# Moving the score gathers of five heads in every chunk from SyncE's DMA queue to GpSimd's

## The chip, the cores and the metric

The kernel runs on one core of one Trainium2 chip. The metric is the device time of one execution in microseconds. Three runs before the change gave a median of 945.39 us (945.13 to 953.41).

## What is computed

Attention with a mixing of the heads before and after the softmax ("talking heads"), and behind it a gated feed-forward layer. Cut to what matters:

```python
batch, n_heads, seq, head_dim = 4, 12, 448, 64        # q, k, v in float32
scores = matmul(q, k.T) / sqrt(head_dim)
scores = einsum('bhij,hg->bgij', scores, w_pre)       # mixes the 12 heads
attn   = exp(scores - max(scores)); attn = attn / (sum(attn) + 1e-09)
attn   = einsum('bhij,hg->bgij', attn, w_post)        # mixes them again
x      = matmul(attn, v)  ->  (batch * seq, 768)
xn = x / rms(x) * rms_g
out = (silu(xn @ w_gate) * (xn @ w_val)) @ w_out      # 768 -> 1536 -> 768
```

## The kernel before, in words

The program is one long list of instructions whose order is written out by hand (the function `part_a` for attention, `part_b` for the feed-forward layer). Each engine takes its instructions strictly in that order and waits on semaphores for what it needs.

Attention is cut into 16 chunks `n`, four for each batch element, of 120 query rows each (100 in every fourth). Each chunk is worked off in 6 steps (5 in every fourth), 92 steps in all. A chunk passes through these stages:

- `qk_mm(n, hp)`, L123: TensorE multiplies q and k for a pair of heads into two PSUM tiles.
- `qk_evac(n, hp, j)`, L126 to L150: the scores of head h = 2 hp + j are copied from PSUM to an SBUF tile `st` (8 buffers), for the even head by ScalarE (L136) and for the odd one by VectorE (L134). Then a DMA, the *gather*, moves `st` into `r`, the tile of the whole chunk (three such tiles, used in turn): the 120 score rows of a head go to 10 partitions, 13 apart, 12 rows to each. So the 12 heads of a group of query rows come to stand on neighbouring partitions, where a matmul can mix them. A gather moves 10 x 12 x 448 floats (210 KB; 175 KB in the chunks of 100 rows). Head 11 takes two gathers of half that size, since it stands on other rows in the second half of the partitions. That makes 13 gathers a chunk.
- `premix(n, p)`, L158: TensorE mixes the heads out of `r` into the PSUM tiles `sp`. The first premix of a chunk needs all 13 gathers.
- `rowmax` (L164, VectorE) writes `nm`, `expo` (L171, ScalarE) writes `e`.
- `norm(n, p)`, L174 to L183: VectorE makes the reciprocals `rp` (L180), then GpSimd scales the post-mixing weights with them: two small TENSOR_SCALAR a step, which write `wn`.
- `postmix` (L197) multiplies `e` by `wn` into `pm`, one step later, and `evac_a` (L210, L212) copies that out.
- `av_mm` (L230), `av_copy` (L240, ScalarE), then `x_sum` (L249 to L259), five GpSimd operations twice a chunk, and `x_store` (L264), a DMA on SyncE's queue.

In one step t, TensorE takes premix(t), one `qk_mm` of the next chunk, postmix(t-1) and one `av_mm` of the chunk before. GpSimd takes, in this order: the jobs of the step (the q loads of L103 and the k loads of L96, which it issues as DMAs), the `wn` of step t, then `x_sum` where there is one. The six head pairs of chunk n + 1 are spread over the steps from two before the first of chunk n to three before the first of chunk n + 1, one pair a step (two in the first of them where chunk n has only 5 steps).

The line that picks a gather's queue is L149. For chunk 0 (n = 0) it deals the gathers out over three queues. For all others, n = 1 to 15, it takes `nc.sync`: 195 gathers, of which 75 are those of heads 1, 3, 5, 7 and 9.

Of the kernel before, what the change touches and what calls it, by code (L numbers as in the profile page):

```python
# [16 lines left out]
B, H, S, D = 4, 12, 448, 64  # L17
# [19 lines left out]
def attention_moe(ctx: ExitStack, tc, q, k, v, wpre, wpost, mask, ident, wgv, wo, rms_g, out):  # L37
    nc = tc.nc
# [87 lines left out]
    def qk_evac(n, hp, j):  # L126
        h, np_ = 2 * hp + j, PAIRS[n % NC]
        ps = qps[n, hp][j]
        if n or h >= 8:
            st = pq.tile([128, S], F32, name="st", tag="st", bufs=8)  # L130
        else:
            st = pro.tile([128, S], F32, name="st", tag="st", bufs=8)
        if j:
            nc.vector.tensor_copy(st, ps[:, :S])  # L134
        else:
            nc.scalar.activation(st, ps[:, :S], AF.Copy)  # L136
        for i, (lo, hi) in enumerate(((0, EARLY), (EARLY, 2 * np_)) if n == 0 else ((0, 2 * np_),)):
            w, at_ = RH * (hi - lo), 2 * RH * lo
            if h < H - 1:
                parts = [(h, 2 * RH, at_, 2 * w)]  # L140
            else:
                parts = [(h, RH, at_, w), (64, RH, at_ + w, w)]
            for row, k_, src, many in parts:
                dst = rt[n][row : row + (k_ - 1) * GAP + 1 : GAP, lo:hi]
                if i:
                    held.append((dst, st[src : src + many]))
                else:
                    turn = h if row < H else h + 1
                    eng = nc.sync if n or turn % 2 else nc.gpsimd if turn % 4 == 2 else nc.scalar  # L149
                    eng.dma_start(dst, st[src : src + many])  # L150

    def premix(n, p):
# [202 lines left out]
    def part_a(extra):  # L355
# [9 lines left out]
        for hp in range(H // 2):  # L365
            qk_mm(0, hp)
            for j in range(2):
                qk_evac(0, hp, j)
            if hp == 4:
                setup()  # L370
# [5 lines left out]
        for t in range(T + 24):  # L376
# [25 lines left out]
            for a in qk_at[t]:  # L402
                for j in range(2):
                    qk_evac(*a, j)
# [404 lines left out]
```

## Time and profile before

| what | value |
|---|---|
| time, median of 3 runs | 945.39 us |
| time of the profiled execution | 946.1 us |
| its span, first to last instruction | 944.3 us |
| TensorE (PE) busy | 869.3 us, 92% of the span |
| VectorE (DVE) busy | 551.4 us, 58% |
| GpSimd (POOL) busy | 383.9 us, 41% |
| ScalarE (ACT) busy | 344.1 us, 36% |
| mean DMA rate | 136 GB/s |

The time of the profiled execution is 1.8 us longer than its span (what lies around the first and last instruction) and 0.7 us above the median of the runs. In the rows, PE is the row of the matmuls and PEld that of the weight loads, which overlap them. SPq is SyncE's own queue, whose instructions are mostly DMA issues. The idle time of an engine stands in brackets with what ended it; "issue" there means that nothing the profile shows was waited for. Attention takes about the first 390 us.

### The profile page before, as it was taken

Reading aid. Unit: us, or ns where it says so; the run is one execution under the profiler, and the core shown is the slowest. Engines: PE = TensorE matmul, PEld = TensorE weight load, DVE = VectorE, ACT = ScalarE, POOL = GpSimd, SP = SyncE. Lnnn points to the kernel's source line nnn. Section 1 sums busy time; section 2 is a strip of 40 time slices with the busy share of each in tenths; the row PEclk is TensorE's granted clock in tenths of the full one; section 3 lists DMA queues with packets and bytes.
Section 4 is the critical chain, followed back from the end, with each engine's and each line's share of the span. In section 5 each row is a group of like instructions: output and inputs, shape, how many; then the busy total and the mean of one; then the engine's idle time right before and its main releaser. Section 6 shows DMA issues by size and latency. Waiting matters only on the chain.

```text
span 944.3 us, 29156 instructions
## 1 busy us (share of the span) xinstructions
PE 869.3 (92%) x12344; PEld 735.4 (78%) x12344; DVE 551.4 (58%) x959; ACT 344.1 (36%) x806; POOL 383.9 (41%) x531
## 2 busy tenths in 40 slices
PE   4798888898898897789999999999999989999998
PEld 1476666576666675678999999999999969999997
DVE  4576677777766674449545664459989868211100
ACT  2566665666666676621211111111111223311200
POOL 4335444444544436634554444444656613000000
PEclk8999999999999999899999999999999989999999
DMA  7765676667655743452321222314332364532010
GB/s 202 203 179 169 187 201 189 195 188 220 187 176 173 205 119 115 140 166 73 107 99 51 82 96 96 106 48 146 130 130 89 123 214 143 190 105 88 30 39 30
DMA packets 72765, 128.18 MB, mean 136 GB/s; under 512 B 19975, under 2 KB 62213, under 8 KB 72635
## 3 DMA queue, kind: packets, MB, share of 16 engines
q1 hardware_dynamic: 68342, 113.53, 38.7%
q0 software_dynamic: 3616, 12.02, 4.6%
q8 instruction: 97, 1.59, 0.7%
q10 hardware_dynamic: 677, 0.77, 0.3%
q14 instruction: 33, 0.27, 0.1%
HBM read 63.77 MB, written 22.95 MB: 92 GB/s over the span
## 4 chain that ended last, share of the span: by engine, by line
PE 62%; DVE 15%; DMA 8%; issue 6%; POOL 5%; ACT 3%; SPq 1%; DVEq 0%; POOLq 0%; ACTq 0%
PE pm L197 6%; PE po L521 6%; PE po L522 6%; PE po L520 6%; PE sp L158 6%; PE av L230 5%; PE qk L123 4%; PE pv L521 4%; PE pv L520 4%; PE pg L522 3%; PE pv L522 3%; PE pg L521 3%; PE pg L520 3%; DMA r<-st 3%; DVE wa L425 3%
## 5 line engine op out<-in xcount | busy, mean ns | idle before, releaser
L171 ACT ACTIVATE e<-sp,nm 128x448 f32<-128x448 f32 x180 | 112.6, 631 | 120.2 <-DVE nm L164 120.2
L197 PEld LDWEIGHTS pm<-wn,e 60*64 60x64 f32 x5152 | 112.1, 134 | 56.4 <-POOL wn L183 26.8
L164 DVE TENSOR_REDUCE nm<-sp 128x1 f32<-128x448 f32 x180 | 104.1, 619 | 73.7 <-PE sp L158 70.3
L197 PE MATMUL pm<-wn,e 60*64 60x60 f32 x5152 | 112.8, 221 | 20.9 <-issue 11.9
L183 POOL TENSOR_SCALAR wn<-wk,rp 128x60 f32<-128x60 f32 x180 | 55.1, 318 | 185.2 <-DVE rp L180 172.7
L158 PE MATMUL sp<-r,wk_pre 64*64 64x448 f32 x720 | 107.9, 557 | 20.2 <-DMA r<-st 10.8
L123 PE MATMUL qk<-k,q 64*64 64x448 f32 x768 | 111.6, 560 | 13.3 <-ACT st L136 8.4
L230 PE MATMUL av<-a,v 64*64 64x120 f32 (+3 forms) x3072 | 98.9, 251 | 9.5 <-issue 6.5
L230 PEld LDWEIGHTS av<-a,v 64*64 64x64 f32 x3072 | 87.6, 134 | 13.2 <-issue 9.7
L520 PE MATMUL pg<-x,wh 128*128 128x448 f32 x264 | 97.0, 367 | 0.0
L520 PE MATMUL pv<-x,wh 128*128 128x448 f32 x264 | 96.7, 366 | 0.0
L521 PE MATMUL pv<-x,wh 128*128 128x448 f32 x264 | 96.7, 366 | 0.0
L522 PE MATMUL pg<-x,wl 128*128 128x448 f32 x264 | 96.7, 366 | 0.0
L522 PE MATMUL pv<-x,wl 128*128 128x448 f32 x264 | 96.6, 366 | 0.0
L521 PE MATMUL pg<-x,wh 128*128 128x448 f32 x264 | 96.6, 366 | 0.0
L453 POOL TENSOR_TENSOR wl<-wc,wh 128x768 fp32r<-128x768 f32 x26 | 49.6, 1907 | 110.0 <-ACT wh L452 110.0
L452 ACT ACTIVATE wh<-wc 128x768 fp32r<-128x768 f32 x26 | 22.0, 847 | 193.2 <-DVE wc L428 193.2
L551 POOL TENSOR_TENSOR g<-g,u 128x448 f32<-128x448 f32 x48 | 62.0, 1292 | 62.6 <-DVE u L550 51.1
L123 PEld LDWEIGHTS qk<-k,q 64*64 64x64 f32 x768 | 43.1, 137 | 49.1 <-ACT st L136 20.7
L504 DVE TENSOR_TENSOR x<-hraw,x 128x448 fp32r<-128x448 f32 x48 | 33.1, 730 | 78.8 <-ACT x L503 78.7
L210 DVE COPY a<-pm 128x420 f32<-128x420 f32 x92 | 54.9, 597 | 30.5 <-PE pm L197 30.1
L134 DVE COPY st<-qk 128x448 f32<-128x448 f32 x96 | 59.1, 616 | 12.6 <-PE qk L123 12.3
(126 smaller groups left out, 1729.9 us busy)
## 6 DMA issues: line engine op xcount, KB each, us to landing
r<-st SPq DMA_DIRECT2D x121, 210.0 KB
wraw<-in_wgv SPq DMA_DIRECT2D x20, 768.0 KB
hd<-sg SPq DMA_DIRECT2D x48, 224.0 KB
hraw<-hd SPq DMA_DIRECT2D x48, 224.0 KB
wraw<-in_wo SPq DMA_DIRECT2D x12, 768.0 KB
r<-st SPq DMA_DIRECT2D x44, 175.0 KB
v<-in_v SPq DMA_DIRECT2D x24, 256.0 KB
q<-in_q POOLq DMA_DIRECT2D x28, 192.0 KB, 4.7
```

Source lines behind the costliest of these rows:

```text
L123: nc.tensor.matmul(ps[j][m, :S], qt[n][sl, hp, m], kt[n // NC, hp][sl], start=True, stop=True)
L134: nc.vector.tensor_copy(st, ps[:, :S])
L158: nc.tensor.matmul(o, wk_pre[sl], rt[n][sl, 2 * p + v_], start=True, stop=True)
L164: nc.vector.tensor_reduce(t, ps[:, :S], AX.X, ALU.max, negate=True)
L171: nc.scalar.activation(e, ps[:, :S], AF.Exp, bias=nmx.pop((n, p, u)), accum_out=sm[n, p][:, u : u + 1])
L183: nc.gpsimd.tensor_scalar(wn[n, p][:, u], wk, r[:, u : u + 1], 1.0, ALU.mult, ALU.mult)
L197: nc.tensor.matmul(o, e[u_][sl, j : j + JT], w[sl, u_], start=True, stop=True)
L230: nc.tensor.matmul(x, vt[b, hp][sl, j, c_], a, start=(c_ == 0), stop=(c_ == JC - 1))
L520: nc.tensor.matmul(ps, a, xh[:, kk], start=(i == 0), stop=False)
L521: nc.tensor.matmul(ps, a, xl_[:, kk], start=False, stop=False)
L522: nc.tensor.matmul(ps, a2, xh[:, kk], start=False, stop=(i == n - 1))
L551: nc.gpsimd.tensor_tensor(g, g, u, ALU.mult)
```

## The change

Gathers of chunks 1 to 15 whose head is odd and below 11 (`j` is 1 and `row` is below 11) are issued by GpSimd. All others stay on SyncE's queue, and chunk 0 is as it was.

```diff
                     turn = h if row < H else h + 1
-                    eng = nc.sync if n or turn % 2 else nc.gpsimd if turn % 4 == 2 else nc.scalar
+                    if n:
+                        eng = nc.gpsimd if j and row < H - 1 else nc.sync
+                    else:
+                        eng = nc.sync if turn % 2 else nc.gpsimd if turn % 4 == 2 else nc.scalar
                     eng.dma_start(dst, st[src : src + many])
```

The new lines push everything behind them down by three: L150 is L153 in the kernel after, L183 is L186, L249 is L252. The order of work on TensorE, VectorE and ScalarE is the same in both kernels.

On GpSimd, in the last three steps of chunk 1, around the first `x_sum` of the program (r_112 is the tile of chunk 3, k_1 and k_2 are key tiles of the next batch element, xt and sum belong to chunk 0's output), before:

```order
L96 DMA k_1_883<-in_k 128x448
L183 TENSOR_SCALAR wn<-wk,rp 128x60 x4
L249 TENSOR_TENSOR xt_980<-xt_980,xt_981 128x360
L250 TENSOR_TENSOR xt_981<-xt_980 128x360
L254 TENSOR_TENSOR xt_981<-xt_981 128x120
L256 TENSOR_TENSOR sum_1058<-xt_981 128x120
L96 DMA k_2_1061<-in_k 128x448
L183 TENSOR_SCALAR wn<-wk,rp 128x60 x2
```

And after:

```order
L96 DMA k_1_883<-in_k 128x448
L186 TENSOR_SCALAR wn<-wk,rp 128x60 x2
L153 DMA r_112<-st 10x10x448
L186 TENSOR_SCALAR wn<-wk,rp 128x60 x2
L252 TENSOR_TENSOR xt_980<-xt_980,xt_981 128x360
L253 TENSOR_TENSOR xt_981<-xt_980 128x360
L257 TENSOR_TENSOR xt_981<-xt_981 128x120
L259 TENSOR_TENSOR sum_1058<-xt_981 128x120
L96 DMA k_2_1061<-in_k 128x448
L153 DMA r_112<-st 10x10x448
L186 TENSOR_SCALAR wn<-wk,rp 128x60 x2
```

A gather now stands directly ahead of the two `wn` of its step, and behind the `x_sum` and the loads of the step before.

On SyncE's queue, the gathers of chunk 1 (r_113) and the first of chunk 2 (r_114) with the loads of v between them, before:

```order
L150 DMA r_113<-st 10x12x448 x10
L107 DMA v_0_433<-in_v 128x512
L107 DMA v_1_435<-in_v 128x512
L150 DMA r_113<-st 10x12x448
L150 DMA r_113<-st 5x12x448 x2
L107 DMA v_2_505<-in_v 128x512
L107 DMA v_3_507<-in_v 128x512
L150 DMA r_114<-st 10x12x448 x2
```

And after:

```order
L153 DMA r_113<-st 10x12x448 x5
L107 DMA v_0_433<-in_v 128x512
L107 DMA v_1_435<-in_v 128x512
L153 DMA r_113<-st 10x12x448
L153 DMA r_113<-st 5x12x448 x2
L107 DMA v_2_505<-in_v 128x512
L107 DMA v_3_507<-in_v 128x512
L153 DMA r_114<-st 10x12x448
```

Five of the ten whole gathers have gone from the queue; the last three of the chunk (head 10 and the two parts of head 11) stand where they stood, behind two loads of v.

## Rows read from the trace of the kernel before

**Rows 1.** Windows by stage: each engine's busy us (instructions), granted clock, DMA share, GB/s.

```profile
core 0: us, PE busy (x) PEld busy (x) DVE busy (x) ACT busy (x) POOL busy (x), PEclk, DMA share, GB/s
40.00:352.00 312.00, 273.23 (x8413) 209.00 (x8409) 214.95 (x537) 199.99 (x531) 142.62 (x318) 0.99 0.64 184
390.00:944.00 554.00, 540.67 (x2758) 492.48 (x2750) 298.48 (x344) 101.90 (x176) 197.03 (x146) 0.99 0.32 104
```

**Rows 2.** Waits of PE, 40 to 352 us: total us, times, longest.

```profile
PE pm L197 <- issue: 11.3, 12, 2.0
PE av L230 <- issue: 6.3, 8, 2.2
PE sp L158 <- issue: 4.8, 3, 2.1
PE pm L197 <- POOL wn L183: 3.3, 7, 1.0
PE sp L158 <- DMA r<-st: 3.2, 3, 1.2
PE sp L158 <- DMA v<-in_v: 2.6, 1, 2.6
```

**Rows 3.** Waits of SyncE's queue, 40 to 352 us, the longest three.

```profile
SPq L150 <- ACT a L212: 108.7, 55, 4.4
SPq L150 <- ACT xt L240: 35.9, 15, 4.7
SPq L150 <- DVE nm L164: 21.3, 41, 1.0
```

**Rows 4.** Tile r: issues of gathers, ns min/median/max, first and last start.

```profile
L150 SPq DMA_DIRECT2D r<-st x201: 742/756/1676, 7.1 to 352.3; - x101
L150 POOL DMA_DIRECT2D r<-st x3: 556/594/782, 8.9 to 12.9; - x3
```

**Rows 5.** GpSimd's groups, 40 to 352 us: the k loads, busy us, mean ns.

```profile
L96 POOL DMA_DIRECT2D k<-in_k x18 | 10.6, 587 | 0.0
```

**Rows 6.** Timeline of POOL, 180 to 190 us: start, length, work [idle before].

```profile
181.70 0.60 POOL L183 TENSOR_SCALAR wn<-wk,rp 128x60 f32<-128x60 f32 x2 [5.87 <-DVE rp L180]
182.26 0.95 POOL L249 TENSOR_TENSOR xt<-xt,xt 128x360 f32<-128x360 f32 x1
...
185.08 0.59 POOL L96 DMA_DIRECT2D k<-in_k  x1
185.71 0.60 POOL L183 TENSOR_SCALAR wn<-wk,rp 128x60 f32<-128x60 f32 x2
...
188.38 0.60 POOL L183 TENSOR_SCALAR wn<-wk,rp 128x60 f32<-128x60 f32 x2 [1.54 <-DVE rp L180]
```

**Rows 7.** Timeline of DVE, the same stretch.

```profile
183.10 0.62 DVE L134 COPY st<-qk 128x448 f32<-128x448 f32 x1
...
184.41 0.17 DVE L180 RECIPROCAL rp<-t 128x2 f32<-128x2 f32 x1
```

**Rows 8.** Timeline of PE, the same stretch.

```profile
182.52 1.03 PE L197 MATMUL pm<-wn,e 60*64 60x60 f32 x55
...
186.09 1.08 PE L197 MATMUL pm<-wn,e 60*64 60x60 f32 x55 [0.20 <-POOL wn L183]
```

**Rows 9.** Timeline of POOL: first and last of twelve late wn.

```profile
68.15 0.60 POOL L183 TENSOR_SCALAR wn<-wk,rp 128x60 f32<-128x60 f32 x2
...
348.49 0.60 POOL L183 TENSOR_SCALAR wn<-wk,rp 128x60 f32<-128x60 f32 x2
```

**Rows 10.** Timeline of PE: the postmix behind each of these two.

```profile
68.62 1.10 PE L197 MATMUL pm<-wn,e 60*64 60x60 f32 x51
...
348.86 1.08 PE L197 MATMUL pm<-wn,e 60*64 60x60 f32 x55
```

**Rows 11.** Chain that ended last, 36 to 47 us: start, us, what.

```profile
37.55 8.16 DMA r<-st
```

**Rows 12.** Timeline of PE, 37 to 46 us: chunk 1's first premix.

```profile
43.81 0.93 PE L158 MATMUL sp<-r,wk_pre 64*64 64x448 f32 x2 [2.65 <-DMA v<-in_v]
```

**Rows 13.** Timeline of SyncE's queue, up to 75 us: chunk 1's last gathers.

```profile
23.49 10.10 SPq L150 DMA_DIRECT2D r<-st  x10
33.63 1.72 SPq L107 DMA_DIRECT2D v<-in_v  x2
35.86 2.43 SPq L150 DMA_DIRECT2D r<-st  x3
```

## The prediction

> **What bounds the kernel now.** I read the windows by stage first, then the waits of PE, then the timelines of POOL, DVE and PE side by side. The windows show that the change can act in one stage only: from 390 us to the end PE is busy 540.67 of 554 us and no gather runs there [rows 1]. In the 312 us from 40 to 352, where nearly all the moved gathers are issued (the last gather of all starts at 352.3 [rows 4]), PE is busy 273.23 us, so some 39 us of idle time is all there is to win. DMA is at 0.64 of its 16 engines there, POOL is busy 142.62 us [rows 1].
>
> The waits of PE say what that idle time is. 22.4 us in 23 waits (11.3 + 6.3 + 4.8) end in "issue", nothing that the profile shows; 3.3 us in 7 end when POOL has made `wn`; 3.2 us in 3 end with a gather, and 2.6 us in one are put down to a load of v [rows 2]. That last one is chunk 1's first premix [rows 12], which reads no v: I count it as gathers, since the chain of waits has a gather in flight from 37.55 us for 8.16 us just there [rows 11]. So PE waits 5.8 us for gathers in this stage, and 3.3 us for POOL.
>
> SyncE's queue is not short of time. It waits 108.7 + 35.9 + 21.3 us at gathers for work of ACT and DVE [rows 3], more than half the stage; a gather costs it 756 ns to issue [rows 4].
>
> POOL has a pattern that matters more. In most steps it sits idle until DVE has made the reciprocals, as before the `wn` at 181.70 (5.87 us) and 188.38 (1.54 us). In the step behind an `x_sum` it does not: the `wn` at 185.71 starts without idle time, straight behind the sums (from 182.26) and a load of k [rows 6], 1.1 us after the reciprocal was done (184.41 + 0.17) [rows 7], and PE has to wait for it [rows 8].
>
> **What the change removes.** 75 issues of some 756 ns leave SyncE's queue, 57 us [rows 4]. Since that queue waits for data far longer than this, I cost the removal at nothing by itself. At chunk 1, the one place where the queue runs packed, ten gathers take it 10.10 us to 33.59; it then issues two loads of v and still waits 0.5 us, until 35.86, for the scores of head 10 [rows 13]. So the last gathers of the chunk cannot start earlier for being behind five instead of ten. What can get shorter is their way: 5 of a chunk's 13 gathers go through another queue. The bounds are no gain and all 5.8 us of PE's waits for gathers; I take the share of the gathers moved, 5/13 of 5.8, which is 2.2 us.
>
> The Trainium skill speaks against any such gain: "DMA: Bandwidth & Descriptors", section "Issuing engines are not separate DMA queues", says that transfers run on the same 16 DMA engines whichever engine issued them, and that another issuer saves only the time of issuing. No row before shows a full gather from POOL. By that rule this term is nothing, and the sum below would be 5.0 us slower instead of 2.8.
>
> **What it adds on POOL.** An issue of a DMA holds POOL for 587 ns with k loads of 224 KB [rows 5], and for 556 to 782 ns (594 in the middle) with the three half-sized gathers of chunk 0 [rows 4]. No full gather from POOL is in the trace. The lower bound is 556 ns, the upper bound twice the longest of the half-sized, 1.56 us; I take 0.59 us, as the k loads are of the same size as a gather.
>
> The gather also waits, for DVE's copy of `st`. Queued behind it on POOL are the two `wn` of the step, any `x_sum` and the next loads; PE waits for the `wn`. In an ordinary step this costs nothing. The copy of `st` ends at 183.72, the reciprocal at 184.58, and a `wn` starts some 0.1 to 0.2 us after that [rows 6, 7]: about 1.0 us in which POOL has nothing to do, against 0.59. Even past it there is a little room: PE took the `wn` of 181.70 at 182.52, 0.82 us after its start [rows 6, 8], where 0.38 would have done (185.71 to 186.09).
>
> In the step behind an `x_sum` there is no such gap. Of the 79 steps of this stage, 19 have a `wn` that starts within 0.1 us of the work before it on POOL. Three of them get no gather (head pair 5 is due there, which stays with SyncE). Four are taken by PE only 0.85 to 2.0 us after their start, so 0.59 us more finds room there. Twelve are left whose `wn` PE takes 0.37 to 0.47 us after the start, as fast as it can [rows 9, 10]. There the gather's 0.59 us stands in full between the sums and the `wn`, and PE's postmix starts later by it: 12 x 0.59 = 7.1 us.
>
> Not all of it reaches the end. PE has 23 "issue" waits in 312 us, one per 13.6 us; a delay in the step ahead of one (a step is 312 / 79 = 3.9 us) only shortens it. I take 3.9 / 13.6, about 0.3, as absorbed: 7.1 x 0.7 = 5.0 us. In the first 40 us POOL gets chunk 1's five gathers; PE there waits at chunk 1's premix anyway [rows 12], which hides a few tenths in the `wn` of chunk 0.
>
> **The sum.** 946.1 us of the profiled execution + 5.0 - 2.2 = 948.9. Its time is 0.7 us above the median of the runs (945.4), so I predict 945.4 + 2.8 = 948.2 us. A measurement of this kernel tells about 1% (9.5 us) from no change, so this is within it.
>
> **Rivals.**
> *Nothing is left.* The late `wn` are absorbed more often than I reckon, or PE gets back all 5.8 us of its waits for gathers. For it: every gather that leaves the queue also leaves the way of head 11's two, which come last. Against it: the twelve rows where PE takes `wn` at once. Time 945.4 + 5.0 - 5.8 = 944.6, or less with more absorbed.
> *POOL becomes the limit.* A full gather costs POOL not 0.59 but, by its size, twice the longest half-sized one, 1.56 us. The gap of an ordinary step is about 1.0 us, and PE leaves about 0.4 more, so this decides from about 1.4 us an issue on. Then the twelve late steps cost 12 x 1.56 x 0.7 = 13.1 us and the some fifty ordinary ones about 0.15 us each, 7.5 us: 945.4 + 20.6 - 2.2 = 963.8. For it: the one issue of 782 ns. Against it: the k loads, at 587 ns for as many bytes.
> *The transfers get room.* At a share of 0.64 [rows 1] the DMA engines are often busy, and a gather from 10 partitions to 120 or back may load some engines more than others, which no view here shows. If sending five of 13 another way evens that out, PE's 5.8 us for gathers go, and with them half of the 22.4 us of "issue", should those be code that arrives late for the same reason: 945.4 + 5.0 - 5.8 - 11.2 = 933.4. For it: the 8.16 us that a gather was in flight [rows 11]. Against it: "issue" waits have no cause in the profile. The Trainium skill has a rule for it ("DMA: Bandwidth & Descriptors", section "Why a DMA increments its semaphore by 16 and not by 1"): queues of SP put a transfer of k shares on the lowest-numbered k engines, GpSimd's on k engines from a cursor that goes round. No row before shows single engines.
>
> **Chances.** My forecast 0.57, nothing left 0.22, POOL the limit 0.13, room for the transfers 0.08. The forecast's own range is 942 to 952.5 (the 7.1 us from a third to all, the gain from 5.8 us to none). For 8 in 10 I go from 940 to 957, the lower end on the side of the third rival, the upper one what an issue of about 1.2 us would make (12 x 1.2 = 14.4 us, less the gain). Faster by over 1% (below 936) takes most of the third rival, 0.06; slower (above 954.8) the second, 0.13; the rest, 0.81, is within.
>
> **What would show it.** In the profile after, POOL should have some 75 more DMA issues of about 0.59 us; PE's waits for `wn` in the stage should grow from 3.3 to near 10 us, at the steps behind an `x_sum`; PE's waits for gathers should shrink from 5.8 to some 3.6 us; the stage should end about 3 us later and the rest stay. I am wrong if an issue costs POOL above 1 us, if `wn` waits appear in ordinary steps, or if "issue" on PE moves by more than 5 us.

## The result and the profile after

The changed kernel takes 959.22 us (median of 20 runs, 946.87 to 968.40), the kernel before on the same chip 947.56 us. The ratio is 1.0122, 95% interval 1.0088 to 1.0157: slower by 1.2%, some 11.6 us. The forecast was 2.8 us slower; its range reached to 957.

Single runs of one kernel spread by 6 to 22 us, and part of that is TensorE's mean granted clock, which each run reports. So beside each ratio I give a difference "at equal clock": over 301 runs of all kernels below, a straight line puts 7.7 us (+-1.2) on each 0.01 of clock, the rest spreads by 3.4 us, and the kernels' means are compared along that line. The changed kernel stands at +11.4 +-1.6 us by it. (A change that itself lowers the clock is flattered by this; where that matters I say so. The ratios leave out the runs over 1.5% above the fastest of their kernel, while the line takes all 301; without those runs no difference moves by more than 1.7 us, except that of `loads_sp_memset`, which loses three of its six runs and goes to -7.8 +-3.7.)

The waits of PE in the stage, 40 to 365 us since the last gather now starts at 364.3 (total us, times, longest), answer to [rows 2]:

```profile
PE av L233 <- issue: 12.9, 11, 2.2
PE pm L200 <- issue: 9.4, 10, 2.4
PE pm L200 <- POOL wn L186: 9.0, 10, 1.5
PE qk L123 <- ACT st L136: 5.5, 3, 1.8
PE sp L161 <- DMA v<-in_v: 2.9, 3, 2.3
PE qk L123 <- issue: 1.3, 1, 1.3
...
PE sp L161 <- DMA wraw<-in_wgv: 0.7, 1, 0.7
...
PE sp L161 <- issue: 0.2, 1, 0.2
PE sp L161 <- DMA r<-st: 0.2, 1, 0.2
```

Of the kernel before, beside [rows 2], one more "issue" wait:

```profile
PE qk L123 <- issue: 0.8, 1, 0.8
```

Waits for `wn` rose from 3.3 to 9.0 us, all ten of them in steps where a gather stands behind an `x_sum`. Waits on transfers fell from 5.8 to 3.8 us (2.9 + 0.7 + 0.2); two kernels below that move no gather, memset_pool and memset_early, have 3.7 and 2.2 us, so the fall need not come from the change. "Issue" stands at 23.8 (before 23.2, the 22.4 of the prediction and the 0.8 at `qk`). Read this way, every step of the prediction seems to come out. Yet the stage ends later by far more than 3 us. The windows answer to [rows 1], the stage stretched to where it ends now:

```profile
core 0: us, PE busy (x) PEld busy (x) DVE busy (x) ACT busy (x) POOL busy (x), PEclk, DMA share, GB/s
...
40.00:365.00 325.00, 280.85 (x8439) 211.42 (x8439) 216.10 (x541) 201.69 (x534) 188.12 (x390) 0.98 0.64 178
```

The same work of the stage takes PE 13 us more than in the 312 us before. From chunk 1's first `wn` (51.3 us before, 51.2 after) to the last step ahead of the last gather (351.1 and 363.9) I get 299.9 and 312.7 us; what follows takes 593.2 and 593.6 us. Of the 12.8 us, PE's idle time makes 6.8 (35.0 to 41.8). Another 5.1 is clock, which fell to one half (1.2 of 2.4 GHz) three times, each time behind an "issue" wait of about 2 us, and not once in this stretch of the profile before. One such fall in the windows, the first at full clock with PE hardly busy:

```profile
118.00:121.00 3.00, 0.59 (x33) 0.45 (x30) 1.02 (x2) 1.77 (x5) 0.64 (x1) 0.99 0.91 266
121.00:124.40 3.40, 3.40 (x70) 3.07 (x73) 0.83 (x3) 0.61 (x1) 1.18 (x3) 0.51 0.50 145
124.40:128.00 3.60, 3.60 (x115) 2.69 (x108) 2.90 (x7) 2.20 (x6) 3.29 (x7) 1.00 0.26 76
```

That share is mostly chance: over the runs the mean clock is 0.9763 against 0.9778, worth 1.2 us.

Tile r on GpSimd, and that engine's groups in the stage (busy us, mean ns, idle before), answer to [rows 4] and [rows 5]:

```profile
L153 SPq DMA_DIRECT2D r<-st x126: 748/781/1647, 7.1 to 364.3; - x126
L153 POOL DMA_DIRECT2D r<-st x78: 553/620/782, 8.9 to 360.6; - x78
```

```profile
L153 POOL DMA_DIRECT2D r<-st x70 | 43.9, 627 | 77.9 <-DVE st L134 75.5 <-issue 1.5 <-DVE t L181 0.2
...
L96 POOL DMA_DIRECT2D k<-in_k x18 | 11.1, 617 | 0.1
```

75 more issues of 0.63 us, as reckoned (0.59). GpSimd waits 75.5 us at them for VectorE's copies of `st`, in time that it had. A late step looks like [rows 6] with one more line (start, length, work):

```profile
68.33 0.43 POOL L259 TENSOR_TENSOR sum<-xt 128x120 f32<-128x120 f32 x1
68.70 0.62 POOL L96 DMA_DIRECT2D k<-in_k  x1
69.32 0.61 POOL L153 DMA_DIRECT2D r<-st  x1
69.97 0.60 POOL L186 TENSOR_SCALAR wn<-wk,rp 128x60 f32<-128x60 f32 x2
```

The queues at work (packets, MB, share of 16 engines' span), first of the kernel before, then after:

```profile
q1 hardware_dynamic: 68342, 113.53, 38.7%
q0 software_dynamic: 3616, 12.02, 4.6%
q8 instruction: 97, 1.59, 0.7%
```

```profile
q1 hardware_dynamic: 58992, 98.12, 33.3%
q0 software_dynamic: 9616, 27.45, 10.3%
q8 instruction: 97, 1.59, 0.7%
```

q1 is SyncE's queue, q0 GpSimd's: 15.4 MB went over. The last line, 97 packets of 16 KB, will matter.

### The profile page after: what moved, and what is told of

The parts are those of the page before. It is cut to its first block, busy times and chain, and to the rows that moved or that the text cites. A ratio compares the mean times of both kernels' runs of the same rounds, so it can differ in the third digit from the quotient of the medians.

```text
span 957.5 us, 29206 instructions
## 1 busy us (share of the span) xinstructions
PE 875.9 (91%) x12344; PEld 737.6 (77%) x12344; DVE 552.3 (58%) x959; ACT 345.0 (36%) x806; POOL 430.3 (45%) x606
## 4 chain that ended last, share of the span: by engine, by line
PE 63%; DVE 13%; POOL 7%; issue 7%; DMA 7%; ACT 2%; SPq 0%; DVEq 0%; POOLq 0%; ACTq 0%
PE pm L200 6%; PE po L524 6%; PE po L525 6%; PE po L523 6%; PE sp L161 5%; PE av L233 5%; PE qk L123 4%; PE pg L523 4%; PE pv L523 4%; PE pg L525 4%; PE pv L525 4%; PE pv L524 4%; PE pg L524 4%; DVE wa L428 2%; DMA wraw<-in_wgv 2%
## 5 line engine op out<-in xcount | busy, mean ns | idle before, releaser
L200 PEld LDWEIGHTS pm<-wn,e 60*64 60x64 f32 x5152 | 109.7, 136 | 69.5 <-POOL wn L186 39.3
L153 POOL DMA_DIRECT2D r<-st x78 | 48.8, 626 | 91.6 <-DVE st L134 76.4
L186 POOL TENSOR_SCALAR wn<-wk,rp 128x60 f32<-128x60 f32 x180 | 54.7, 313 | 62.6 <-DVE rp L183 56.2
```

Of the source, the lines that this page charges most:

```text
L186: nc.gpsimd.tensor_scalar(wn[n, p][:, u], wk, r[:, u : u + 1], 1.0, ALU.mult, ALU.mult)
L200: nc.tensor.matmul(o, e[u_][sl, j : j + JT], w[sl, u_], start=True, stop=True)
```

## The experiments

Three theories stood at first. **A**: GpSimd's time at the issues holds up `wn`, as predicted, only oftener. **B**: a gather that goes through GpSimd's queue costs something by its way, whatever time GpSimd has. **C**: the change also alters which of the eight `st` buffers a tile gets, since the pool hands out the one that is free first. In the built programs a buffer comes back after exactly 8 tiles before, after 4 to 11 in the changed kernel. "Ordinary" places are 52 of the 75, "late" ones the 23 behind an `x_sum`.

All runs, with their interval and the difference at equal clock (95%):

| kernel | ratio to before | at equal clock, us |
|---|---|---|
| again (before itself) | 1.0004 (0.9970 to 1.0038) | +0.7 +-2.0 |
| the change | 1.0122 (1.0088 to 1.0157) | +11.4 +-1.6 |
| early_only | 1.0092 (1.0060 to 1.0123) | +9.1 +-2.2 |
| late_only | 1.0364 (1.0319 to 1.0410) | +29.7 +-2.9 |
| memset_pool | 1.0030 (0.9991 to 1.0068) | +3.8 +-2.0 |
| after_rot | 1.0087 (1.0053 to 1.0120) | +9.0 +-2.6 |
| before_slots_of_after | 0.9992 (0.9959 to 1.0025) | +0.1 +-2.0 |
| early_rot | 1.0067 (1.0036 to 1.0098) | +7.5 +-2.0 |
| late_rot | 1.0084 (1.0049 to 1.0119) | +7.3 +-2.0 |
| memset_early | 1.0013 (0.9987 to 1.0040) | +0.2 +-2.0 |
| copy_early | 1.0309 (1.0262 to 1.0357) | +20.8 +-3.1 |
| loads_sp | 0.9979 (0.9947 to 1.0012) | -5.1 +-2.0 |
| after_loads_sp | 1.0064 (1.0024 to 1.0104) | +7.0 +-2.0 |
| both_early | 1.0119 (1.0078 to 1.0159) | +12.7 +-2.8 |
| scalar_early | 1.0037 (1.0005 to 1.0069) | -0.3 +-2.1 |
| loads_sp_2 | 0.9962 (0.9921 to 1.0003) | -4.7 +-2.0 |
| loads_sp_memset | 0.9868 (0.9787 to 0.9949), by the medians of all runs 0.9975 | -3.4 +-2.8 |

**again** is the kernel before, unchanged, as a measure of the measuring.

> The kernel before, unchanged, timed against itself. It gives the width of no change, and the mean granted clock of the kernel before over several runs, beside the 0.977 of the profile after (0.983 in the profile before). Theory A (GpSimd's time: a gather issued between the sums of x_sum and wn makes PE wait): ratio 1.000 within 0.004, and a mean clock near 0.983, since the clock's falls in the kernel after are a consequence of PE standing still more often. Theory B (the gathers' way through GpSimd's queue: it disturbs the code loads behind PE's issue waits or the landing of gathers, wherever the gather is issued): the same ratio. If the clock of the kernel before is also 0.977 over its runs, the part of the loss that I now put down to the clock in the profile after (some 5 of 13 us) is no part of the change at all.

1.0004: what follows can be told apart to about 0.3%.

**early_only** moves the gathers of ordinary steps alone, **late_only** those behind an `x_sum` alone (with `and behind_sums[0]`):

```diff
+    behind_sums = [False]
...
+                        eng = nc.gpsimd if j and row < H - 1 and not behind_sums[0] else nc.sync
...
+            behind_sums[0] = bool(done)
```

> Of the 75 moved gathers the 52 stay on GpSimd that stand in a step not behind an x_sum; the 23 in a step behind an x_sum go back to SyncE's queue. Theory A: PE's waits for wn from 52 to 365 us, 9.1 us in the profile after, go back to some 3.3 us as before, and the ratio to the kernel before is 1.000 to 1.003. Theory B: the loss goes with the number of gathers on GpSimd's queue, 52/75 of 11.6 us, which is 8 us or a ratio of 1.0085.

> The counterpart: only the 23 gathers in a step behind an x_sum are issued by GpSimd, the other 52 by SyncE. Theory A: nearly the whole loss, PE's waits for wn 8 to 10 us and a ratio of 1.006 to 1.012. Theory B: 23/75 of 11.6 us, 3.6 us or a ratio of 1.004, with waits for wn at the same 8 to 10 us but made up for elsewhere.

The 52 ordinary gathers, which I had costed at nothing, bring 9.1 us. The 23 late ones alone bring more than the whole change, and their profile says why. First PE's waits from 40 to 390 us, then VectorE's, then VectorE's timeline at one such place:

```profile
PE qk L124 <- DVE st L135: 19.3, 10, 3.5
PE pm L201 <- POOL wn L187: 15.1, 23, 1.6
```

```profile
DVE st L135 <- DMA r<-st: 44.4, 11, 6.3
```

```profile
118.52 1.16 DVE L168 TENSOR_REDUCE nm<-sp 128x1 f32<-128x448 f32 x2 [1.41 <-PE sp L162]
123.97 0.62 DVE L135 COPY st<-qk 128x448 f32<-128x448 f32 x1 [4.29 <-DMA r<-st]
```

VectorE, which waits for a buffer of `st` not once in the kernel before and once, 0.3 us, in the changed one, waits 11 times here until the gather before has read its buffer: this copy stands 4.29 us for a gather that GpSimd issued at 117.83, behind the sums. In this kernel 13 tiles get the buffer of the tile two before them. That is theory C, at its worst in a kernel that nobody asked for.

**memset_pool** keeps all gathers on SyncE and gives GpSimd a write of a spare tile, about 0.59 us, at the 75 places:

```diff
+    pad = [cst.tile([128, 576], F32, name="idle_pad")]
...
+                    if n and j and row < H - 1:
+                        nc.gpsimd.memset(pad[0], 0.0)
```

> All gathers are issued by SyncE as before. GpSimd instead does a memset of a spare tile of 128 x 576 (some 0.6 us, as long as it issues a gather) at each of the 75 places where the kernel after issues one. So GpSimd's time is that of the kernel after and the gathers' way that of the kernel before. Theory A: the loss of the kernel after, ratio 1.006 to 1.013, PE's waits for wn 8 to 10 us. Theory B: none of it beyond what the waits for wn make directly, a ratio below 1.006, with the clock as in the kernel before.

+3.8 us. In its profile PE waits 7.0 us for `wn` (40 to 354 us), near the 9.0 of the change:

```profile
PE pm L200 <- POOL wn L186: 7.0, 10, 1.3
```

So theory A's waits are there and cost about what I had forecast for them (5.0); they are a third of the loss.

**after_rot, before_slots_of_after, early_rot, late_rot** settle C. The first, third and fourth are the change, early_only and late_only with the buffers strictly in turn, the second is the kernel before with every `st` tile in the buffer that it has in the changed kernel:

```diff
-            st = pq.tile([128, S], F32, name="st", tag="st", bufs=8)
+            st = pq.tile([128, S], F32, name="st", tag=f"st{(12 * n + h) % 8}", bufs=1)
```

> The kernel after, with the eight st buffers taken strictly in turn (each tile names its buffer). In the kernel before each st tile takes the buffer of eight tiles ago; in the kernel after, the pool hands them out otherwise, and a tile takes the buffer of 4 to 11 tiles ago. Theory C (the changed order of the buffers): what is left is GpSimd's time alone, 1.003 as with the memsets in the place of the gathers. Theory B (the gathers' way through GpSimd's queue): 1.012 as the kernel after.

> The kernel before, all gathers on SyncE's queue, but every st tile takes the buffer that it has in the kernel after. Theory C: the part of the loss that the memsets do not make, 1.006 to 1.010. Theory B: no change, within 0.004 of 1.000.

> The 52 gathers in steps not behind an x_sum on GpSimd, the other 23 on SyncE, and the st buffers strictly in turn. Without the turn this was 1.0092, with a tile taking the buffer of two tiles ago in three places. Theory C: within 0.003 of 1.000. Theory B: 52/75 of what the memsets leave unexplained (8.8 us), 1.006.

> The 23 gathers in steps behind an x_sum on GpSimd, the other 52 on SyncE, and the st buffers strictly in turn. Without the turn this was 1.0364, with DVE waiting 44.4 us for a gather that was only just issued, since 13 tiles of head 5 or 7 took the buffer of the head before. Theory C: those waits go and the ratio falls to 1.002 to 1.006, the direct cost of GpSimd's time (1.003 with the memsets). Theory B alone could not explain 34 us with 23 gathers and would leave most of it.

late_only falls from 29.7 to 7.3 us with the buffers in turn: C is real there, 22 us. But the buffers of the changed kernel cost the kernel before nothing (+0.1), and the change in turn loses 9.0 in place of 11.4, within the errors: C explains little or nothing of the result. early_rot stays at +7.5.

**memset_early** is the memset at the 52 ordinary places alone, **copy_early** a transfer of a gather's size from a spare tile to a spare tile at the same places, issued by GpSimd, with no gather moved:

```diff
+                    if n and j and row < H - 1 and not behind_sums[0]:
+                        nc.gpsimd.dma_start(copies[at_copy[0] % 4][: 2 * w], pad[0][: 2 * w])
+                        at_copy[0] += 1
```

> All gathers on SyncE as before; GpSimd writes a spare 128x576 tile (about 0.6 us) at the 52 places where a kernel that moved only the gathers of ordinary steps, with the st buffers taken in turn, issued a gather there and came to 1.0067. Theory A (GpSimd's time costs): 1.005 to 1.008 here as well. Theory B (the gather's way through GpSimd's queue costs, not the time on the engine): 0.999 to 1.003.

> All gathers on SyncE as before; at the same 52 places GpSimd issues a DMA of the size of a gather from a spare constant tile to a spare tile that nobody reads. Theory B1 (a transfer that GpSimd issues costs by itself, whoever waits for it): 1.005 to 1.008. Theory B2 (the loss comes from the gather itself going that way, what premix waits for): 0.999 to 1.003. Theory A: as the memset at the same 52 places.

memset_early, +0.2: in ordinary steps GpSimd's time is free, as predicted, and the 7.5 us of early_rot are the gathers' way. (A memset does not wait for VectorE's copy as a gather does; but in early_rot's profile PE waits only 1.7 us for `wn` and 3.6 for transfers from 40 to 361 us, no more than before, so that wait is not what costs.) Between the two memset kernels lies the price of the late places, 3.6 us. late_rot, with 7.3 us, lies above what theory C gave it, and 3.7 +-3.5 us of it are not GpSimd's time. copy_early overshot every expectation, since it adds 10.8 MB to what the stage moves; as a test of the way alone it is spoilt. But it shows how sensitive the stage is to transfers:

```profile
PE pm L205 <- issue: 15.9, 14, 2.6
PE sp L166 <- DMA r<-st: 15.4, 6, 8.6
```

(PE's waits from 50 to 350 us. The longest, 8.6 us, is chunk 1's first premix, which in the kernel before ends ahead of this stretch; the other 6.8 us compare with 2.1 there.) Not only the gathers come late, "issue" grows as well, to 30.7 us from 23.3. That sent me to the packets of q8. In 16 kernels, the two of this case among them, I set the end of every "issue" wait of PE from 50 to 350 us beside them: 353 of 354 (those over 0.1 us) end 1.15 to 2.41 us behind the landing of one of these 16 KB packets, among them all 25 of the kernel before. The packets come once every 256 instructions of PE (a line through their starts in the kernel before gives 255.8; the 97 packets of 256 make 24832, and its profile has 24939 instructions of PE, weight loads and waits included). So "issue" on PE is a wait for its own code, which arrives by DMA among the gathers.

**loads_sp** and **after_loads_sp** move the 44 loads of q and k from GpSimd to SyncE, in the kernel before and in the changed one:

```diff
-        (nc.gpsimd if b else nc.sync).dma_start(t, k[b, :, hp])
+        nc.sync.dma_start(t, k[b, :, hp])
...
-    def load_q(n, hp, many=3, eng=nc.gpsimd):
+    def load_q(n, hp, many=3, eng=nc.sync):
```

> The kernel before with the 44 loads of q and k that GpSimd issues moved to SyncE, no gather moved. Theory B1: each transfer off GpSimd's queue gives back what one on it costs (0.0067/52 of the time each), so 0.993 to 0.996. Theory B2: 0.998 to 1.002. Theory A: GpSimd waits 3.3 us shorter at most, 0.997 to 1.000.

> The changed kernel with the loads of q and k moved to SyncE as well: GpSimd issues 75 gathers and no loads in place of 44. Theory B1 (counts transfers through GpSimd's queue): 31 more than before in place of 75, 1.003 to 1.006. Theory B2: as the changed kernel, 1.008 to 1.014. Theory A (time of issues behind the sums): 1.006 to 1.010, as the long steps behind an x_sum lose the load's issue too.

Taking transfers off GpSimd's queue helps, -5.1 us. With the loads gone from both, the change costs 12.1 us (7.0 + 5.1), as much as before.

**both_early and scalar_early.** Theory **D**, new here: two queues at once keep more DMA engines busy, whichever the second. both_early sends even and odd heads of ordinary steps through GpSimd's queue, scalar_early the 52 through ScalarE's (in early_rot's line `j and` is left out, 116 gathers, and `nc.gpsimd` becomes `nc.scalar`).

> In ordinary steps (none behind an x_sum) the gathers of even and odd heads alike go out from GpSimd's queue, the others from SyncE's, st buffers in turn: about twice the gathers of the kernel that moved 52 and came to 1.0067, but a step's two gathers stand in one queue again. Theory B (each gather costs by going through GpSimd's queue): about 1.013, PE's waits called issue 28 us or more between 50 and 350 us. Theory D (two queues at once keep more DMA engines busy, and PE's code packets come late behind them): time with 11 or more packets under way falls back from 159 towards 128 us of 50 to 345, issue waits near 21 us, and beyond waits for wn (GpSimd issues two in a step, at 0.6 us each, with about 1.0 us of room) 0.999 to 1.004.

> The 52 gathers of ordinary steps go out from ScalarE's queue in place of GpSimd's, st buffers in turn. Theory B (GpSimd's queue in particular costs): 0.999 to 1.003 beyond what ScalarE's own wait for VectorE's st copy costs (its next exp then starts late, seen as waits of GpSimd and PE behind e). Theory D (two queues at once): time with 11 or more packets under way near 159 us again, PE's waits called issue 25 us or more, 1.005 or more.

scalar_early costs nothing at equal clock; its mean clock is low (0.9732), so by the plain ratio it costs 0.4%, and the two readings can't be told apart for certain. both_early loses 12.7 us, but differently. PE's waits, 40 to 365 us:

```profile
PE pm L201 <- POOL wn L187: 17.4, 30, 1.3
PE av L234 <- issue: 12.4, 9, 3.0
PE pm L201 <- issue: 3.9, 6, 1.4
```

Two issues, 1.2 us, no longer fit into the gap of about 1.0 us ahead of `wn`, and 14 us more of waits for `wn` are enough for its loss; "issue" did not grow to the 28 us that B asked for. Neither theory as I had put it survives: D fails on the number of packets under way (next section), which is not raised by ScalarE's queue and does not fall back with both on GpSimd's.

**loads_sp_memset** leaves GpSimd a memset of 0.59 us where each load was, **loads_sp_2** is loads_sp again beside it:

```diff
+        if b:
+            nc.gpsimd.memset(pad[0], 0.0)
...
+        if n:
+            nc.gpsimd.memset(pad[0], 0.0)
```

> The kernel before with the 44 loads of q and k moved from GpSimd's queue to SyncE's, and a write of a spare 128x576 tile (0.59 us, what the issue of a load takes) left on GpSimd at each of their places: GpSimd's time as before, its queue without the loads. Theory B (what goes through GpSimd's queue costs, 0.11 to 0.14 us a transfer, by the two kernels that moved 52 gathers, 7.5 us, and 44 loads, 5.0 us, at equal clock): 0.993 to 0.997. Theory A (GpSimd's time): the gain of the kernel that moved the loads is gone, 0.999 to 1.003.

> The same kernel as in the earlier run that moved the 44 loads of q and k to SyncE (0.9979, interval 0.9947 to 1.0012), beside the one with GpSimd's time put back. Theory B and theory A both: 0.993 to 0.998; it is the candidate that may beat both kernels.

-4.7 us again, and -3.4 +-2.8 with GpSimd's time put back: most of the gain seems to be the queue, but the interval is too wide to share it out. At equal clock loads_sp is the best version here. Its two intervals just reach 1 (upper ends 1.0012 and 1.0003), and at equal clock it is 4.9 us faster than before in the mean of both runs, 16 us faster than the change.

## Why the prediction was wrong

**The step that failed** is the gain from the gathers' way: "The bounds are no gain and all 5.8 us of PE's waits for gathers; I take the share of the gathers moved". Its bounds had no loss in them. Measured by early_rot against memset_early, the way of the 52 ordinary gathers costs 7.3 us (7.5 - 0.2, +-2.8). With that in place of -2.2 the sum is 5.0 + 7.3 = 12.3 us, against 11.4 measured. That it comes so near is partly luck: the way of the 23 late gathers, 3.7 +-3.5 us by late_rot and the memsets, is not in it. The gather waits themselves did not grow (3.8 us, 3.6 forecast); the price was paid elsewhere. So the size of the failed term is shown; why the way costs this much is not, as the counts below tell.

**The step that held** is GpSimd's time. The issue took 0.63 us (0.59 taken), ordinary steps were free (+0.2), `wn` waits went from 3.3 to 9.0 us (near 10 forecast), all of them behind an `x_sum`, and the late places cost 3.6 +-2.8 us by the memsets, 5.0 forecast.

**Where the way costs.** Three counts over the packets of the traces belong together; the first two are shown, the third is not clear of chance, so the chain is an argument and not a proof.

First, I counted how many packets are under way at once from 50 to 345 us, q8 left out. The bytes are alike (52.0 to 55.4 MB) in these kernels, the time with 11 or more packets is not (late_only, 48 MB, and copy_early, 59 MB, are left out):

| gathers | us of 295 with 11 or more packets |
|---|---|
| on SyncE: before, again, before_slots_of_after | 128, 126, 128 |
| the same with memsets or moved loads (five kernels) | 124, 126, 127, 124, 130 |
| 52 on ScalarE: scalar_early | 131 |
| 23 on GpSimd: late_rot | 129 |
| 52 to 116 on GpSimd: early_only, early_rot, the change, after_rot, after_loads_sp, both_early | 155, 159, 158, 165, 164, 151 |

So it is not a second queue that spreads the traffic but GpSimd's: SyncE's packets of 1792 bytes alone stand at exactly 10 in 40 of 300 us before and at 11 or more in only 13, however many gathers wait behind each other. A gather writes 10 partitions. The Trainium skill has the rule that I had given to the third rival ("DMA: Bandwidth & Descriptors", section "Why a DMA increments its semaphore by 16 and not by 1"): SyncE's and ScalarE's queues put a transfer of 10 shares on the ten lowest-numbered engines, GpSimd's on ten from a cursor that goes round. These counts agree with it, though the trace does not tell single engines apart. The same page's section "Issuing engines are not separate DMA queues" would make the way cost nothing; here the measurement, 7.3 us, decides.

Second, what that does to PE's code. A code packet is due at a fixed place in PE's program, one in 256 instructions; I counted how much later than that place, at its earliest in the kernel before, each packet starts, and how many packets of q0 and q1 were under way, on average, in the microsecond behind it. Over 18 kernels and 1139 code packets (the 113 with fewer than 5 beside them start 0.68 to 0.90 us late):

| packets under way when code is due | code packets | start late by, us (mean) |
|---|---|---|
| 5 to 8 | 123 | 0.68 |
| 8 to 11 | 404 | 1.02 |
| 11 to 13 | 171 | 1.40 |
| 13 to 17 | 328 | 1.80 |

The differences between these rows are what counts: if the place is put some tens of instructions earlier or later, all rows move together and 0.8 to 1.1 us remain between the first and the last.

Third, what PE loses. In the nine kernels with gathers on SyncE or ScalarE code starts late by 1.16 us on average and PE's "issue" waits come to 18.9 us in the stage (10.5 to 23.4); in the six with 52 or more on GpSimd by 1.34 us and 23.2 us (16.5 to 28.8). The difference, 4.3 us, would be more than half of the 7.3, but single profiles of either group spread by about 4 us, which makes it 4.3 +-4.8 (95%). It is not clear of chance: before and again alone stand at 23.4 and 21.5 us, and both_early, with 116 gathers on GpSimd, at 16.5. What single waits look like is plain. In the profile after, the wait that ends at 76.67 follows a code packet that took 2.16 us and landed 1.44 us ahead of it (start, length, work):

```profile
76.67 0.55 PE L233 MATMUL av<-a,v 64*64 64x120 f32 x16 [1.77 <-issue]
```

Not in a wait at all: PE's busy time in the stage, less what the clock took, is 2.1 us longer in the same six and late_rot than in the nine (267.8 against 265.7), which no row explains.

**The rivals.** "The transfers get room" had named the spreading by GpSimd's queue, which the first count bears out, and forecast a gain from it; the time went the other way. That the room for the gathers is taken from PE's code is argued from the counts and the rule, not shown. "POOL becomes the limit" came nearest in time (963.8) for a reason that did not occur, as an issue took 0.63 us and not 1.56. The sign of wrongness that I had named, "issue" moving by more than 5 us, did not show in the one profile (+0.6), and could hardly have told: profiles of kernels with the gathers on SyncE differ by more among themselves (10.5 to 23.4), and even the means of several leave the difference open.

**What stays open.** The parts do not add up exactly: 52 gathers alone cost 7.5 us and 23 alone 7.3 with the buffers in turn, both together 9.0 +-2.6. Why the loads, whose moving changed nothing in the count of packets (124 to 130 us without them on GpSimd's queue, 126 to 128 with), gave back 4.9 us is at most partly explained by PE's `wn` waits, which fell from 3.3 to 0.3 and 0.2 us. late_rot loses its 7.3 us with 129 us of 11 or more packets, as in the kernel before, so the 3.7 us of it that are not GpSimd's time have another source, if they are more than noise. And no run changed how a gather is spread on one and the same queue. On GpSimd's queue its packets are three times as long as well (5376 bytes in place of 1792) and small ones of 12 bytes come with them; both are rivals of the spreading, and no run separates the three. So the spreading is shown to go with the loss of the 52 ordinary gathers, not to cause it.

## What to carry to other kernels

Before moving a DMA to another engine's queue, ask not only what its issue costs there but what its transfer will run beside: here the issue was nearly free and the way was not. "Issue" waits of a busy TensorE can be its own code arriving among the transfers, so bound every edit of the DMA traffic on that side too, with a loss in the range. When an experiment moves a transfer, pin the buffers of its pool: a rotation that shifted by itself cost 22 us and would have been read as the price of the move.

## What the runs showed that I had not expected

- PE's code comes in 16 KB packets, one for every 256 of its instructions, each taking about 1.09 us to move (63 of them from 50 to 345 us before), and 353 of 354 "issue" waits of PE end just behind one. They come to 10.5 to 32.5 us in the stage of these kernels, the most in copy_early.
- The same gather is made of packets of 1792 bytes at 91 to 103 ns on SyncE's and ScalarE's queue, and of 5376 bytes at 306 to 330 ns on GpSimd's (means of the kernels), with packets of 12 bytes beside them (1429 from 50 to 345 us in the changed kernel, none before).
- 52 idle transfers of a gather's size, which nobody waits for, cost 29 us (1.0309) and took the mean clock from 0.978 to 0.967.
- The mean granted clock of one and the same kernel varied from run to run enough to move its time by several us, 7.7 us for each 0.01.
